# Linear attention with a gated FFN on one core: M3 of two token tiles at the second level, M4's results stored by accumulating DMA

## The chip, the cores and the metric

The kernel runs on one core of a Trainium2 chip. A core has five engines that run their own instruction streams: TensorE (PE, matrix products into PSUM; PEld is its loading of weights), VectorE (DVE), ScalarE (ACT), GpSimd (POOL) and SyncE (SP), which here only issues DMAs. DMAs can be issued by SP, ACT and POOL and run on 16 DMA engines. The metric is the time of one execution on the device in microseconds (us), as the median of the runs shown; a second, profiled execution gives the trace that the readings come from. Times in the trace count from the start of its span.

## The reference

Two blocks are computed from x (2048 tokens of 1024, bfloat16), and one gates the other:

```python
xn = layernorm(x)
q, k, v = split(xn @ wqkv)              # 32 heads of 32
pq, pk  = phi(q), phi(k)                # phi(t) = (t + 1 if t > 0 else exp(t)) + 1e-6
o = (pq @ sum(pk v^T)) / (pq . sum(pk) + 1e-6)
s = o @ wo                              # linear attention
f = (silu(xn @ w_gate) * (xn @ w_up)) @ w_down     # 1024 -> 3584 -> 1024
out = x + s * silu(f)
```

The change concerns the last line and the product with w_down in it.

## The kernel before

The tokens are handled in blocks of 512 (TB), a block in four token tiles of 128 (P). First come the layer norm, the attention and s, which is kept in DRAM as s_dram. Then the FFN runs in two passes of 1024 tokens each (`passes`, the later tokens first). In a pass, gate and up are computed for 14 groups of 256 hidden units (NFG), and then the product with w_down.

All FFN products use the Strassen-Winograd scheme, which replaces the eight block products of a 2x2 by 2x2 block product with seven, M1 to M7, at the price of sums of blocks before and after. For w_down, the rows of a block are 512 tokens, its columns 512 outputs (CW), and the inner dimension is halved by the parity of 128-unit chunks. Tiles 0 to 3 are the first 512 tokens of a pass, tiles 4 to 7 the second; output half 0 is the first 512 columns, half 1 the second. In the last pass, `emit_down_m` (L1459) computes the seven products one after another in the order 1, 2, 6, 7, 5, 4, 3 (M_ORDER). M1, M2, M4 and M7 are done by the same scheme once more, "at the second level" (`l2_M`, L1529): for a pair of token tiles, seven products of seven matmuls with 128 tokens and 256 columns each, in place of 2 x 14 matmuls with 512 columns. Their weight sums were made earlier and lie in DRAM (l2_drams). M6, M5 and M3 are done directly, tile by tile (`prod_t`, L1493: 14 matmuls of 512 columns).

The second level within `l2_M` runs like this, for both tile pairs r = 0, 1: product 1 for both pairs into one half of a PSUM bank; a copy by ACT of each into a second bank (L1538); product 2 onto the first; products 5 and 6; a second copy (L1546); product 7; DVE adds; a `fill()`, which is work of another product for PE; product 4; product 3; DVE adds.

The end of the last pass, which the change rewrites, is:

```python
go(l2_M(4, quads(h, 1, 1), KB, done4, fill3, True))   # fill3: flush(); M3 of tile 0 (out3)
out3(1, 2)                                            # M3 of tile 1, then two stores
ps = banks(2)                                         # two banks for tile 3, preloaded by ACT (L1669)
out3(2, 3)                                            # M3 of tile 2, then three stores
flush()
```

`out3` puts M3 of a tile onto M5 in the same PSUM bank, lets DVE add KA (the running sum of M1, M2, M6 and M7 that output half 1 of tiles 0 to 3 needs), and ACT apply silu. Tile 3 is last and is split into 384 and 128 columns, so that its end is short: there M5 was added to KA early, ACT copies KA into the banks (L1669), and M3 accumulates onto it.

A finished piece of 128 tokens by 512 columns is stored by `fin` (L1219): DVE multiplies silu's result by s (L1223) and adds x (L1224), and SP stores it (L1225). The piece's x and s were loaded into an io tile by `io_load` (L1204; L1214 for x, L1215 for s), which each `fin` calls for a later piece; fq holds the order. Pieces that wait for their `fin` stand in a queue, and `flush(n)` handles n of them.

The order of instructions on PE, DVE, ACT and POOL is the order in which the code emits them; SP's is written by hand in the sections marked so, and otherwise set by the planner. The weights of the seven products are loaded by SP into eight slots (`load_w`, L240; L255 for second-level weights, L262 for M5, M6 and M3), a slot's load being issued when the product that used the slot before has been read. POOL computes the second-level sums of weights and of M1's and M2's left side (L1149, L1180 to L1183) until 673.8 us and is idle after that. DVE makes the left sums of M7 and M4 (`l2_lhs_r`, L1172 to L1175).

Of the kernel before, what the change touches and what calls it, by code (L numbers as in the profile page):

```python
# [21 lines left out]
def kernel(  # L22
# [11 lines left out]
    nc = tc.nc  # L34
# [919 lines left out]
    with ExitStack() as p3:  # L954
# [8 lines left out]
        def k2(shape, dt, name):  # L963
            return kp.tile(shape, dt, name=name, tag="k2")
# [200 lines left out]

        def l2_lhs_r(M, A, r, eng):
            if not isinstance(A, tuple):
                A = (A[:, 0], A[:, 1])
            v = [a.rearrange("p j (r t n) -> p j r t n", r=2, t=2)[:, :, r] for a in A]
            a11, a12, a21, a22 = v[0][:, :, 0], v[1][:, :, 0], v[0][:, :, 1], v[1][:, :, 1]  # L1170
            s1, s2, s3, s4 = [x[:, :, r] for x in l2_bufs(M)]
            eng.tensor_tensor(out=s1, in0=a21, in1=a22, op=ALU.add)  # L1172
            eng.tensor_tensor(out=s2, in0=s1, in1=a11, op=ALU.subtract)
            eng.tensor_tensor(out=s3, in0=a11, in1=a21, op=ALU.subtract)
            eng.tensor_tensor(out=s4, in0=a12, in1=s2, op=ALU.subtract)  # L1175
# [26 lines left out]
        hold = [False]  # L1202

        def io_load(after=None):  # L1204
            if not fq:
                return
            if hold[0] and after is None:
# [6 lines left out]
            gate([nc.sync.dma_start(out=io[:, 0, :], in_=x2[r0:r0 + P, cc * CW:(cc + 1) * CW]),  # L1214
                  nc.sync.dma_start(out=io[:, 1, :], in_=s_dram[r0:r0 + P, cc * CW:(cc + 1) * CW])],  # L1215
                 after, sync=True)
            io_tiles[key] = io

        def fin(p, t, cc, y, eng1, eng2, out_eng, cols=None):  # L1219
            io = io_tiles[(p, t, cc)]  # L1220
            r0 = p * TB2 + t * P
            cs = cols or slice(0, CW)
            eng1.tensor_tensor(out=y[:, cs], in0=y[:, cs], in1=io[:, 1, cs], op=ALU.mult)  # L1223
# [5 lines left out]
        def emit_down(p, h, base, more_S, next_S):  # L1229
# [152 lines left out]
            for hf in range(2):  # L1382
                t0, t1 = 2 * hf, 2 * hf + 1
                for st in range(NS):
                    if st == 4:
                        flush()
                    if hf == 0:
# [71 lines left out]
        def emit_down_m(p, h, base):  # L1459
# [149 lines left out]

            def done2(t, c):  # L1610
                fins.append((t, 0, silu(c, "g11")))
# [36 lines left out]
            tt(KA[-1], M5[-1], KA[-1])  # L1648
            load(5)

            def out3(t, n=0):
                prod_t(3, t, M5[t], False)
                flush(n)
                c = k2([P, CW], FP32, "c12")[:]
                tt(c, M5[t], KA[t])
                fins.append((t, 1, silu(c, "g12")))

            def done4(t, c):
                fins.append((t + TPB, 0, silu(c, "g21")))

            def fill3():
                flush()
                out3(0)
            go(l2_M(4, quads(h, 1, 1), KB, done4, fill3, True))
            hs_ = [slice(0, 3 * CW // 4), slice(3 * CW // 4, CW)]
            out3(1, 2)
# [3 lines left out]
            out3(2, 3)  # L1670
# [194 lines left out]
```

## Time and profile before

| | |
|---|---|
| Median of 3 runs | 751.8 us (751.67 to 751.89) |
| Profiled execution | 751.77 us, span 750.0 us |
| Instructions in the span | 11301 |
| Granted PE clock | 1.000 |
| PE busy from 736.8 to 746.1 us | 9.29 of 9.30 us |
| PE busy from 746.1 us to the end | 0 |
| DMA share, 736.8 to 746.1 us | 0.37 |

The page has the busy time of each engine, the span in 40 slices, the DMA queues, the chain of work that ended last followed back from the last instruction, the costliest groups of instructions, and the DMA issues. A group's row gives the line, the engine, the operation, its output and inputs with shapes, how often, the busy time, the mean of one, and the engine's idle time before it with what ended it. The time line of a stretch gives start and duration, and merges neighbours of the same kind. Matmul ends are modelled: a matmul of 512 columns is shown with 0.379 us, one of 256 with 0.273, while in a row of them the next starts after about 0.216 and 0.109 us.

### The profile page before, as it was taken

The numbers are of one execution on the slowest core, as the hardware profiler recorded it, in microseconds if no ns is written. First come the engines' busy times: TensorE is split into PE (matmuls) and PEld (weight loads), VectorE is DVE, ScalarE is ACT, GpSimd is POOL, SyncE is SP. The second block draws the span as 40 slices with busy tenths as digits, with TensorE's granted clock in tenths as the row PEclk, the third lists the DMA queues.
The fourth block names the chain that finished last, engine by engine and source line by source line (L and its number), as shares of the span: only waits on it lengthen the run. The fifth ranks groups of instructions, "written<-read, shape, count | busy, mean of one in ns | idle before, by whom it ended". The sixth has DMA issues, their size and how long they took to land.

```text
span 750.0 us, 11301 instructions
## 1 busy us (share of the span) xinstructions
PE 743.4 (99%) x3941; PEld 369.6 (49%) x3941; DVE 587.2 (78%) x1068; ACT 384.0 (51%) x553; POOL 398.2 (53%) x492
## 2 busy tenths in 40 slices
PE   8999999999999999999999999999999999999997
PEld 4544544454454444444444444744444444467664
DVE  6687787887697688888889886587877768688856
ACT  5678767889965666666557411232223232332023
POOL 2435799998540255858586027410767575780000
PEclk9999999999999999999999999999999999999999
DMA  9967799869688668787889418898698888679853
GB/s 319 297 148 149 214 331 308 311 141 285 186 212 276 224 228 289 283 317 288 302 281 391 184 55 294 258 375 283 240 307 304 307 295 312 260 229 317 272 186 99
DMA packets 132473, 194.21 MB, mean 259 GB/s; under 512 B 36432, under 2 KB 106192, under 8 KB 122688
## 3 DMA queue, kind: packets, MB, share of 16 engines
q1 hardware_dynamic: 124224, 159.21, 65.9%
q0 software_dynamic: 6752, 31.79, 11.0%
q10 hardware_dynamic: 1440, 2.49, 1.0%
q8 instruction: 31, 0.51, 0.3%
q14 instruction: 26, 0.21, 0.1%
HBM read 122.68 MB, written 63.44 MB: 248 GB/s over the span
## 4 chain that ended last, share of the span: by engine, by line
PE 96%; DVE 3%; ACT 1%; issue 0%; DVEq 0%; ACTq 0%
PE zw L968 26%; PE kv_ps L556 15%; PE xb L968 13%; PE yb L968 6%; PE q_ps L183 6%; PE dzw L1247 6%; PE dm L1526 6%; PE dm L1490 5%; PE s_ps L776 3%; PE fx L818 2%; PE dy L1247 2%; PE dx L1247 2%; PE dm L1247 1%; PE kvz L578 1%; PE nd L745 1%; PE warm_ps L592 1%
## 5 line engine op out<-in xcount | busy, mean ns | idle before, releaser
L968 PEld LDWEIGHTS <-w_sb 128*128 128x128 f16 (+1 forms) x1568 | 152.2, 98 | 182.7
L968 PE MATMUL xb<-xnT,w_sb 128*128 128x512 bf16 x448 | 115.0, 379 | 0.0
L556 PE MATMUL kv_ps<-wkv_sb,xnT 128*128 128x512 bf16 x512 | 113.7, 379 | 0.6 <-DVE xnT L543 0.3
L968 PE MATMUL zw<-xnT,w_sb 128*128 128x512 bf16 x448 | 105.8, 379 | 0.0
L968 PE MATMUL zw<-S,w_sb 128*128 128x512 f16 x448 | 105.8, 379 | 0.0
L323 POOL TENSOR_TENSOR w_sb<-w_sb 128x512 f16<-128x512 bf16 x42 | 50.2, 1195 | 95.7 <-DVE w_sb L311 51.3
L288 ACT ACTIVATE w_sb<-w_sb 128x2048 bf16<-128x2048 bf16 x42 | 79.9, 1902 | 4.7 <-DMA w_sb<-in_B_w_up_dram 4.7
L556 PEld LDWEIGHTS <-xnT 128*128 128x128 bf16 x512 | 48.3, 98 | 56.0 <-ACT xnT L545 0.8
L1149 POOL TENSOR_TENSOR w_sb<-w_sb 128x512 f16<-128x512 f16 (+3 forms) x48 | 51.4, 1093 | 29.0 <-DMA w_sb<-wd 28.0
L1044 ACT ACTIVATE sg<-cg 128x1024 bf16<-128x1024 f32 x28 | 29.6, 1057 | 57.5 <-DVE cg L1037 57.5
L183 PE MATMUL q_ps<-xnT,wq_sb 128*128 128x512 bf16 x256 | 58.4, 379 | 0.0
L968 PE MATMUL yb<-S,w_sb 128*128 128x512 f16 x224 | 57.4, 378 | 0.0
L1037 DVE SCALAR_TENSOR_TENSOR cg<-zw,rc_all,s 128x1024 f32<-128x1024 f32 x28 | 35.9, 1283 | 24.2 <-PE zw L968 12.6
L996 DVE SCALAR_TENSOR_TENSOR s<-yb,rc_all,s 128x512 f32<-128x512 f32 x42 | 31.4, 749 | 29.3 <-ACT s L995 29.3
L324 POOL TENSOR_TENSOR w_sb<-w_sb 128x512 f16<-128x512 bf16 x42 | 50.4, 1201 | 3.3
L1225 POOL DMA_DIRECT2D out_dram<-io x16 | 8.7, 543 | 79.6 <-DVE io L1224 79.4
L326 POOL TENSOR_TENSOR w_sb<-w_sb 128x512 f16<-128x512 bf16 x42 | 50.3, 1197 | 0.0
L325 POOL TENSOR_TENSOR w_sb<-w_sb 128x512 f16<-128x512 bf16 x42 | 50.2, 1196 | 0.0
L995 ACT ACTIVATE s<-xb,rcl 128x512 f32<-128x512 f32 x14 | 9.6, 687 | 65.3 <-PE xb L968 65.3
L995 ACT ACTIVATE s<-xb,rc_all 128x512 f32<-128x512 f32 x42 | 28.3, 674 | 21.9 <-issue 12.9
L311 DVE TENSOR_SCALAR w_sb<-w_sb,cs_all 128x2048 bf16<-128x2048 bf16 x35 | 36.7, 1048 | 2.8
L183 PEld LDWEIGHTS <-wq_sb 128*128 128x128 bf16 x256 | 24.4, 98 | 27.5
(226 smaller groups left out, 1351.4 us busy)
## 6 DMA issues: line engine op xcount, KB each, us to landing
w_sb<-pk_g SPq DMA_DIRECT2D x27, 1024.0 KB, 7.0
pk_g<-w_sb SPq DMA_DIRECT2D x14, 1024.0 KB, 5.4
w_sb<-pk_u SPq DMA_DIRECT2D x14, 1024.0 KB, 8.7
pk_u<-w_sb POOLq DMA_DIRECT2D x13, 1024.0 KB, 5.4
w_sb<-l SPq DMA_DIRECT2D x12, 896.0 KB, 6.6
l<-w_sb POOLq DMA_DIRECT2D x9, 896.0 KB, 7.7
w_sb<-in_B_w_gate_dram SPq DMA_DIRECT2D x14, 512.0 KB, 6.6
w_sb<-in_B_w_down_dram SPq DMA_DIRECT2D x28, 256.0 KB, 4.7
```

What stands on the lines that cost most here:

```text
L183: nc.tensor.matmul(q_ps[:], lhsT=wq_sb[:, dc, g * P:(g + 1) * P], rhs=xn_ap(dc, btok), start=(dc == 0), stop=(dc == DC - 1))
L288: nc.scalar.activation(out=junk, in_=raw_view(key, t), func=ACT.Square, accum_out=asum[:])
L323: nc.gpsimd.tensor_tensor(out=T1, in0=b12, in1=b11, op=ALU.subtract)
L324: nc.gpsimd.tensor_tensor(out=T2, in0=b22, in1=T1, op=ALU.subtract)
L325: nc.gpsimd.tensor_tensor(out=T3, in0=b22, in1=b12, op=ALU.subtract)
L326: nc.gpsimd.tensor_tensor(out=T4, in0=b21, in1=T2, op=ALU.subtract)
L556: mm = nc.tensor.matmul(kv_ps[:], lhsT=xn_ap(dc, tok), rhs=wkv_sb[:, dc, c * CW:(c + 1) * CW], start=(dc == 0), stop=(dc == DC - 1))
L968: mm = nc.tensor.matmul(out, lhsT=lhs(k), rhs=rhs(k), start=(first and k == 0), stop=(k == HK - 1), skip_group_check=True)
L995: nc.scalar.activation(out=s1[:], in_=x_[:], func=ACT.Copy, scale=rc)
L1149: nc.gpsimd.tensor_tensor(out=b(o_), in0=b(a_), in1=b(b_), op=ALU.subtract)
L1247: nc.tensor.matmul(out, lhsT=lhs, rhs=rhs, start=first, stop=lastk, skip_group_check=True)
L1526: nc.tensor.matmul(out, lhsT=lhs, rhs=w[:, j], start=i == 1 and j == 0, stop=j == NQ - 1, skip_group_check=True)
```

## The change

M3 of tiles 0 and 1 is computed at the second level. Its four sums of weights are made by POOL (`t3_sums`, 28 operations of 128x256), out of the slots into which M3's weights were loaded, into the tiles that held S3. Its four left sums are made by DVE (`l3_sums`) into the room of A11. The products go into the banks of M5 of tiles 0 and 1, so M5 of these tiles is now added to KA by DVE beforehand. Products 1, 5, 2 and 6 stand in `fill3`, product 7 after M4, then M3 of tile 2 directly, then products 4 and 3, and tile 3 last as before.

The four pieces of M4 (output half 0 of tiles 4 to 7) are no longer added to x by DVE: x is copied once, DRAM to DRAM, to these rows of out (`acc_base`), and POOL stores each piece with a DMA that accumulates onto out. Their io tiles load s alone.

```diff
--- before.py
+++ after.py
@@ -1163,6 +1163,10 @@
             v = A[:, :, j].rearrange("p k (r t n) -> p k r t n", r=2, t=2)
             return v[:, 0, :, 0], v[:, 1, :, 0], v[:, 0, :, 1], v[:, 1, :, 1]
 
+        def l2_quad4(A):
+            v = [A[:, k].rearrange("p j (r t n) -> p j r t n", r=2, t=2) for k in range(2)]
+            return v[0][:, :, :, 0], v[1][:, :, :, 0], v[0][:, :, :, 1], v[1][:, :, :, 1]
+
         def l2_lhs_r(M, A, r, eng):
             if not isinstance(A, tuple):
                 A = (A[:, 0], A[:, 1])
@@ -1200,6 +1204,11 @@
 
         io_due = deque()
         hold = [False]
+        acc = [(passes[-1], t + TPB, 0) for t in range(TPB)]
+
+        def acc_base():
+            r0 = passes[-1] * TB2 + TB
+            nc.sync.dma_start(out=out2[r0:r0 + TB, 0:CW], in_=x2[r0:r0 + TB, 0:CW])
 
         def io_load(after=None):
             if not fq:
@@ -1211,15 +1220,21 @@
             r0 = p * TB2 + t * P
             pool, tg = (sp, "S%d" % len(fq)) if len(fq) < 3 else (iop, "io")
             io = pool.tile([P, 2, CW], BF16, name="io", tag=tg)
-            gate([nc.sync.dma_start(out=io[:, 0, :], in_=x2[r0:r0 + P, cc * CW:(cc + 1) * CW]),
-                  nc.sync.dma_start(out=io[:, 1, :], in_=s_dram[r0:r0 + P, cc * CW:(cc + 1) * CW])],
-                 after, sync=True)
+            cs = slice(cc * CW, (cc + 1) * CW)
+            loads = [] if key in acc else [nc.sync.dma_start(out=io[:, 0, :], in_=x2[r0:r0 + P, cs])]
+            loads.append(nc.sync.dma_start(out=io[:, 1, :], in_=s_dram[r0:r0 + P, cs]))
+            gate(loads, after, sync=True)
             io_tiles[key] = io
 
         def fin(p, t, cc, y, eng1, eng2, out_eng, cols=None):
             io = io_tiles[(p, t, cc)]
             r0 = p * TB2 + t * P
             cs = cols or slice(0, CW)
+            if (p, t, cc) in acc:
+                eng1.tensor_tensor(out=io[:, 0], in0=y, in1=io[:, 1], op=ALU.mult)
+                nc.gpsimd.dma_start(out=out2[r0:r0 + P, cc * CW:(cc + 1) * CW], in_=io[:, 0], accum_op=ALU.add)
+                io_load()
+                return
             eng1.tensor_tensor(out=y[:, cs], in0=y[:, cs], in1=io[:, 1, cs], op=ALU.mult)
             eng2.tensor_tensor(out=io[:, 0, cs], in0=y[:, cs], in1=io[:, 0, cs], op=ALU.add)
             out_eng.dma_start(out=out2[r0:r0 + P, cc * CW + cs.start:cc * CW + cs.stop], in_=io[:, 0, cs])
@@ -1384,6 +1399,8 @@
                 for st in range(NS):
                     if st == 4:
                         flush()
+                        if hf == 0:
+                            acc_base()
                     if hf == 0:
                         for m in {4: (4,), 8: (5, 6)}.get(st, ()):
                             more_S(m)
@@ -1607,6 +1624,37 @@
                 M5.extend(banks())
                 prod_t(5, 0, M5[0], True)
 
+            T3w = [x[:].rearrange("p j (s n) -> p j s n", s=2) for x in s3_]
+            T3w = dict(zip((5, 6, 7, 4), (T3w[0][:, :, 0], T3w[0][:, :, 1], T3w[1][:, :, 0], T3w[1][:, :, 1])))
+            L3 = A11.bitcast(F16).rearrange("p (j k) (s n) -> p k j s n", k=2, n=P)[:, 0]
+            L3 = dict(zip((5, 6, 7, 3), [L3[:, :, i] for i in range(4)]))
+            Q3 = [v[:, :, 0] for v in l2_quad4(quads(h, 1, 0).bitcast(F16))]
+
+            def w3(j, k, c):
+                return w_of(3, 2 * j + k)[:, c * CH:(c + 1) * CH]
+
+            def t3_sums():
+                for i, k, c, src in ((5, 0, 1, None), (6, 1, 1, 5), (7, 1, 1, None), (4, 1, 0, 6)):
+                    for j in range(NQ):
+                        b_ = w3(j, 0, 0) if i == 5 else w3(j, 0, 1) if i == 7 else T3w[src][:, j]
+                        nc.gpsimd.tensor_tensor(out=T3w[i][:, j], in0=w3(j, k, c), in1=b_, op=ALU.subtract)
+
+            def l3_sums():
+                a11, a12, a21, a22 = Q3
+                tt(L3[5], a21, a22)
+                tt(L3[6], L3[5], a11, ALU.subtract)
+                tt(L3[7], a11, a21, ALU.subtract)
+                tt(L3[3], a12, L3[6], ALU.subtract)
+
+            def l3_p(i):
+                half, y0 = {1: (0, 0), 2: (0, 0), 5: (0, 1), 3: (0, 1), 6: (1, 1), 7: (1, 0), 4: (1, 0)}[i]
+                out = M5[half][:, y0 * CH:(y0 + 1) * CH]
+                for j in range(NQ):
+                    lhs = L3[i] if i in L3 else Q3[{1: 0, 2: 1, 4: 3}[i]]
+                    w = T3w[i][:, j] if i in T3w else w3(j, *{1: (0, 0), 2: (1, 0), 3: (1, 1)}[i])
+                    nc.tensor.matmul(out, lhsT=lhs[:, j], rhs=w, start=i == 1 and j == 0, stop=j == NQ - 1,
+                                     skip_group_check=True)
+
             def done2(t, c):
                 fins.append((t, 0, silu(c, "g11")))
             S3 = tuple(x[:] for x in s3_)
@@ -1645,29 +1693,50 @@
                 fins.append((t + TPB, 1, silu(c, "g22")))
                 if t > 1:
                     flush(1)
-            tt(KA[-1], M5[-1], KA[-1])
             load(5)
-
-            def out3(t, n=0):
-                prod_t(3, t, M5[t], False)
-                flush(n)
-                c = k2([P, CW], FP32, "c12")[:]
-                tt(c, M5[t], KA[t])
-                fins.append((t, 1, silu(c, "g12")))
+            t3_sums()
+            for t in (0, 1, 3):
+                tt(KA[t], M5[t], KA[t])
+            l3_sums()
 
             def done4(t, c):
                 fins.append((t + TPB, 0, silu(c, "g21")))
+            b0, b1 = M5[0:2]
+            lo, hi = slice(0, CH), slice(CH, CW)
 
             def fill3():
                 flush()
-                out3(0)
+                l3_p(1)
+                nc.scalar.copy(out=b1[:, hi], in_=b0[:, lo])
+                l3_p(5)
+                l3_p(2)
+                l3_p(6)
+                nc.scalar.copy(out=b1[:, lo], in_=b1[:, hi])
             go(l2_M(4, quads(h, 1, 1), KB, done4, fill3, True))
             hs_ = [slice(0, 3 * CW // 4), slice(3 * CW // 4, CW)]
-            out3(1, 2)
+            l3_p(7)
+            c1 = k2([P, CW], FP32, "l2c")[:]
+            tt(c1[:, hi], b1[:, lo], KA[1][:, hi])
+            tt(KA[0][:, hi], b1[:, hi], KA[0][:, hi])
+            tt(c1[:, hi], b0[:, hi], c1[:, hi])
+            prod_t(3, 2, M5[2], False)
+            flush(3)
+            c = k2([P, CW], FP32, "c12")[:]
+            tt(c, M5[2], KA[2])
+            g2 = silu(c, "g12")
+            turn[0] += 1
             ps = banks(2)
             for i in range(2):
                 nc.scalar.copy(out=ps[i][:, 0:hs_[i].stop - hs_[i].start], in_=KA[-1][:, hs_[i]])
-            out3(2, 3)
+            l3_p(4)
+            tt(c1[:, lo], b1[:, lo], KA[1][:, lo])
+            g1 = silu(c1, "g12")
+            l3_p(3)
+            flush()
+            c0 = k2([P, CW], FP32, "l2c")[:]
+            tt(c0, b0, KA[0])
+            g0 = silu(c0, "g12")
+            fins.extend([(2, 1, g2), (1, 1, g1), (0, 1, g0)])
             flush()
             t = TPB - 1
             g12 = k2([P, CW], BF16, "g12")[:]
```

## The prediction

> **What bounds the kernel now.** I read the page's busy table first, then the chain of waits over the last 50 us, then the last 35 us engine by engine, because apart from one early copy the change touches only that stretch. The page's first part and the chain, whose columns are start, us, and the work:
>
> ```profile
> PE 743.4 (99%) x3941; PEld 369.6 (49%) x3941; DVE 587.2 (78%) x1068; ACT 384.0 (51%) x553; POOL 398.2 (53%) x492
> ...
> 722.87 0.70 DVE c L1478
> 723.57 0.02 issue
> 723.60 0.72 ACT g L1512
> 724.32 0.28 ACT dm L1538
> 724.60 0.04 issue
> 724.64 6.27 PE dm L1526 x56
> 730.91 3.02 PE dm L1490 x14
> 733.94 3.06 PE dm L1526 x28
> 736.99 8.33 PE dm L1490 x42
> 745.33 0.02 issue
> 745.35 0.59 ACT g L1678
> ```
>
> PE is the path. It leaves it at two places: after 745.33 (silu, multiply, add, store of the last piece: the span ends at 750.0), and once at 722.87, where DVE and then ACT hold PE up. There the copy of M4's first product between two PSUM banks (L1538) stands on ACT behind a silu, that behind a DVE add, and the add waits for the last M5 product. From that product's end (722.85) to PE's next matmul (724.64) are 1.79 us. The chain also gives PE's rates: 14 matmuls of 512 columns take 3.02 us, 28 of 256 take 3.06.
>
> The time line of DVE around 720 and of POOL earlier (start, us of one instruction or group, idle before):
>
> ```profile
> 719.34 0.62 DVE L1175 TENSOR_TENSOR kept<-hT,kept 128x896 f16<-128x896 bf16 x1
> 719.87 0.68 DVE L1478 TENSOR_TENSOR c<-dm,kB 128x512 f32<-128x512 f32 x1
> ...
> 722.87 0.69 DVE L1478 TENSOR_TENSOR c<-dm,kB 128x512 f32<-128x512 f32 x1 [1.53 <-PE dm L1490]
> ```
> ```profile
> 667.41 0.67 POOL L1182 TENSOR_TENSOR w_sb<-hT 128x256 f16<-128x256 bf16 x1
> 668.04 1.44 POOL L1183 TENSOR_TENSOR w_sb<-hT,w_sb 128x256 f16<-128x256 bf16 x1
> 669.45 1.11 POOL L1180 TENSOR_TENSOR kept<-hT 128x256 f16<-128x256 bf16 x1
> ```
> ```profile
> 668.87 4.39 DVE L1478 TENSOR_TENSOR S3h<-hT 128x1024 f16<-128x1024 bf16 x4
> ```
>
> DVE has 1.53 us of slack before the add that holds PE at 722.87, and POOL is idle there. A POOL subtraction of 128x256 takes 0.67 (one per 0.63) alone or beside DVE work that reads PSUM, but 1.1 beside DVE work on two SBUF operands; and those four DVE operations take 1.08 each, where seven of the same size at 681.07, with POOL idle, take 4.29 us, or 0.61 each. So the two engines take turns: 0.61 for DVE, 0.47 for POOL.
>
> **The change part by part.** The sum is made against the profiled execution's 751.77 us (span 750.0, 1.77 around it), 0.03 below the median of 751.8.
>
> *PE work.* M3 of tiles 0 and 1 goes from 28 matmuls of 512 columns (2 x 3.02 = 6.04 us) to 7 x 7 = 49 of 256 (49 / 28 x 3.06 = 5.36). Gain 0.68.
>
> *Wait after M3's product 1.* It goes into one half of bank b0; ACT copies it to b1 (L1710), and the next matmuls, product 5, write b0's other half. In the built order the first load of weights of product 5 waits for ACT: the bank is guarded as a whole. In M4 the same step has two tiles interleaved, so that a second product covers the copy; here there is one tile pair, and nothing. Price: the last matmul of 256 columns lasts 0.27 at a pitch of 0.11, so 0.16 drains; 0.02 to ACT; 0.36 copy (L1546's mean); 0.04 back: 0.58. Bounds 0.28 (PE's idle at 724.36, with cover) and 0.7; I take 0.58, which is built of this very step. The second copy (L1714) has 3.06 us of M4's products after it and costs nothing.
>
> *Wait before the last tile.* The copies of KA into the last tile's two banks (L1730, before L1669) used to stand on ACT at 741.70, ahead of need at 742.87. They now stand behind the silu of tile 2, which waits for the DVE add on tile 2's product, the same three steps as at 722.87. There PE was back 1.79 after the product ended; here the copy is of 384 columns (L1669: 0.47, not 0.36), so 1.90. PE has products 4 and 3 of M3 to do meanwhile: 14 x 0.109 = 1.53, less 0.16 of drain, 1.37. PE stands for 0.53. Bounds 0.1 (a copy that started at once) and 0.9; I take 0.53. Product 4 and product 3 wait for POOL and DVE work that is long done.
>
> *POOL's 28 subtractions (L1640).* Their data land when M3's slots do: the eight loads of L262 are issued from 712.27 to 717.1 and take 4.5 to 5.2 us, so slab 0 is there at about 717.25 and one more every 0.7 us to 721.6. The first seven sums thus fall on DVE's second set of M4's sums (L1172 to L1175, 717.61 to 719.95) and on the two operations of a final store. Taking turns at 0.47 per POOL operation, I step through it: the four sums end at 721.4 instead of 719.9, the store's two operations at 723.3, and the add that had 1.53 us of slack starts at 723.33 instead of 722.87. Silu, copy and PE behind it move as far: 0.46. Bounds 0 (one collision hidden) and 1.1. Going on like this, the sums for products 5, 6, 7 and 4 are complete at 724.0, 730.3, 735.9 and 740.5; PE, on the times of this sum, wants the last of each at 733.2, 734.7, 738.5 and 742.4. POOL is covered by 1.9 us at its tightest, a mean of 0.83 us against 0.90 allowed.
>
> The Trainium skill, "SBUF — State Buffer", section "Who interferes with whom", says that a DVE instruction with two SBUF inputs contends with a GpSimd one that reads SBUF, and that the loser blocks for the whole instruction. The trace agrees on which instructions collide, but its pair takes 1.08, less than the 0.61 + 0.63 of whole blocking; what the sum would be by the rule's letter stands as a rival below.
>
> *DVE's additions.* Two more adds onto KA (0.60 pitch) and four sums of 128x896 (0.54, 1.0 beside POOL) stand in DVE's idle 5.3 us before 730.26; they end at 730.7 and delay M4's adds by half a microsecond, which PE reads only at 734. M4's results lose one of two DVE operations each. In the end three stores instead of two stand between the last-but-one product and the last: 0.60 + 3 x 0.87 = 3.2 us from 0.35 before PE starts the last tile, so done 2.9 after that start (742.87 in the trace), while ACT's silu of the first piece ends 3.1 after it (745.93). Cost 0, with 0.2 to spare.
>
> *DMAs.* SP loses four loads of x and four stores in the tail; nothing waited there for SP. POOL issues four accumulating stores: three behind its last sum at 741, one at about 744, while the last SP store lands near 748.7 + 0.9. Nothing on POOL stands behind them. No row shows an accumulating transfer; POOL's plain stores of the same 128 KB land 2.0 to 6.4 us after issue (median 3.4), and one more read of 128 KB takes 2.6 in this stretch (the loads of x), so 746 to 753; I take 750, at the edge, and count 0. The Trainium skill, "DMA: Bandwidth & Descriptors", section "Rules for kernel authors", says that an accumulate reads its destination and writes it later, which is that added read; no run here shows it yet.
>
> *The copy of x to out.* It is written in the first pass, but the built order has it on SP right after the loads of wq, so at 23 us. 512 KB at the 349 GB/s of that stretch are 1.5 us, or 3.0 if reading and writing share it:
>
> ```profile
> 28.00:30.50 2.50, 2.50 (x19) 1.37 (x18) 2.37 (x5) 2.50 (x6) 2.09 (x6) 1.00 1.10 349
> ...
> 31.50:33.50 2.00, 2.00 (x17) 1.15 (x16) 1.97 (x5) 1.91 (x4) 1.39 (x7) 1.00 0.05 15
> ```
>
> The last two columns are the DMA engines' share and GB/s: full until 30.5, empty from 31.5 to 33.5. The transpose behind it (L530) is issued at 32.39, when DVE is ready, and lands about 3.3 later; PE reads that tile at 38.5 (eight matmuls, 1.73 us, before the next group of L578 at 40.29). 2.8 us of slack against at most 1.5 of delay: cost 0.
>
> *Sum:* -0.68 + 0.58 + 0.53 + 0.46 = +0.89. 751.77 + 0.89 = 752.7, or 0.12% more. From no change, a measurement of this kernel can tell about 0.2%, or 1.5 us: 750.3 to 753.3.
>
> **The rivals.**
>
> *The gain stays.* The copy's wait is shorter than its parts, and the order on ACT does no harm: 751.77 - 0.68 = 751.1. For it: only that such handoffs sometimes overlap. Against it: the built order has both waits. A gain above 1.5 us has no source, since all of M3's saving is 0.68.
>
> *DVE held off for all of each POOL operation*, 0.63 instead of 0.47: the same stepping has the add before M4 start at 724.16 instead of 723.33, 0.83 more, and POOL's last sum end at 743.4, about when PE then wants it: 753.5. For it, the 1.44 us of one POOL row; against it, the 1.08 of the pairs. It is what the Trainium skill's section named above would give.
>
> *POOL late for product 4* (the case on the slower side): if DVE keeps POOL at the 1.07 of the collision rows throughout, 28 take 30.0 us, to 747.2, and PE, which wants the last at 742.4, stands for 4.8: 757.5. It decides from a mean of 0.90 us on. Against it: DVE's work on two SBUF operands fills only 9 of these 24 us (eight sums of 0.54, eight store operations of 0.42, four results of 0.35).
>
> *The accumulating store ends the kernel.* The last, issued at 744, decides if it takes over 5.6 us to land; at 9.0 (6.4 + 2.6) the end moves by 3.4: 756. Against it: plain stores land in 1.8 in this stretch, where DMA is at a third.
>
> **How the numbers follow.** Forecast 0.47 (its own range 752.0 to 753.3), gain stays 0.08, whole blocking 0.18, POOL late 0.11, late store 0.12, something else 0.04. Slower by over 0.2%: 0.18 + 0.11 + 0.12, 0.01 of the forecast's upper edge and half of the rest, 0.44. Faster: 0.02 of the kept gain, should more come with it, and 0.01 of the rest, 0.03. Within: what is left, 0.53. The range from 751.2 to 755.5 takes in the forecast, most of the kept gain, the blocking and the milder half of the late cases.
>
> **What would show it.** PE idle 0.6 after the first seven matmuls of L1655, released by ACT L1710; idle 0.5 before the 384-column matmuls, released by L1730; the DVE add before M4 at about 723.3, and PE's wait there 0.7 instead of 0.28; L1640's POOL rows at 0.83 on average and done by 741. The prediction is wrong if a matmul of L1655 waits for POOL, if SP's last wait is for POOL's queue, or if PE idles near 38.

## The result and the profile after

The changed kernel takes 753.14 us (median of 9 runs, 752.97 to 755.61) where the kernel before takes 751.62 (9 runs, 751.34 to 751.89): a ratio of 1.0025, with an interval of 1.0015 to 1.0036. It is slower by 1.5 us. The forecast was 752.7 us, and the range of 751.2 to 755.5 holds the time; but the likeliest case, less than 0.2% from no change, is just missed by the median, and the interval reaches into it.

The profiled execution takes 753.14 us with a span of 751.1, so 2.04 lie around the span; before, it was 751.77, 750.0 and 1.77. First the page's busy times, the trace's waits of PE over the last 50 us, and the time line of PE around each of them (start, us, and in brackets the idle time before with what ended it):

```profile
PE 743.0 (99%) x3962; PEld 371.4 (49%) x3962; DVE 595.6 (79%) x1073; ACT 384.9 (51%) x555; POOL 424.4 (57%) x524
```
```profile
PE dm L1543 <- ACT dm L1555: 0.8, 1, 0.8
PE dm L1655 <- DVE kB L1495: 0.5, 1, 0.5
PE dm L1507 <- ACT dm L1730: 0.4, 1, 0.4
```
```profile
722.73 1.69 PE L1543 MATMUL dm<-w_sb,hT 128*128 128x256 f16 x14
725.23 1.03 PE L1543 MATMUL dm<-w_sb,hT 128*128 128x256 f16 x8 [0.81 <-ACT dm L1555]
...
731.34 0.93 PE L1655 MATMUL dm<-w_sb,hT 128*128 128x256 bf16 x7
732.81 0.93 PE L1655 MATMUL dm<-S3h,hT 128*128 128x256 f16 x7 [0.54 <-DVE kB L1495]
733.57 0.93 PE L1655 MATMUL dm<-w_sb,hT 128*128 128x256 bf16 x7
...
742.71 0.93 PE L1655 MATMUL dm<-w_sb,hT 128*128 128x256 bf16 x7
744.08 2.71 PE L1507 MATMUL dm<-w_sb,hT 128*128 128x384 bf16 x19 [0.45 <-ACT dm L1730]
```

In the kernel before, PE had one wait here, of 0.28 us:

```profile
724.64 1.69 PE L1526 MATMUL dm<-w_sb,hT 128*128 128x256 f16 x14 [0.28 <-ACT dm L1538]
```

Now there are three, and they are the three of the forecast: before M4, after M3's product 1, and before the last tile. The rows give their price from start to start. Seven matmuls of 256 columns that follow each other take 0.76 (732.81 to 733.57). Product 5 starts 1.47 after product 1, so 0.71 are lost; the last tile starts 1.37 after product 3, so 0.61; and M4's fourteen matmuls take 2.50 to the next start instead of 1.97 (722.67 to 724.64), so 0.53. That is 1.85; M3 itself saves 0.69, as two later runs show; PE is 0.06 late already at 722.7. So the last tile should start 1.22 later, and the trace has it at 744.08 instead of 742.87.

The chain of waits (start, us) returns to PE through the same add, silu and copy as before, 0.6 later, and leaves it once more ahead of the last tile. (Before, the chain left PE only at 722.85, when the add's product was done; now it leaves PE at 713.08 and runs along DVE's queue from there. Between the two pieces shown it also names DVE additions for the wait after product 1, which the part on the prediction takes up.)

```profile
723.48 0.69 DVE c L1495
...
724.19 0.72 ACT g L1529
724.91 0.28 ACT dm L1555
...
725.23 6.27 PE dm L1543 x56
...
742.14 0.70 DVE c L1495
...
742.93 0.45 ACT g L1529
...
743.56 0.48 ACT dm L1730
...
744.08 2.45 PE dm L1507 x14
```

Both pieces have one form: a copy that PE needs stands on ACT behind a silu, and the silu waits for a DVE add that PE does not need. (L1529 is the silu, L1555 and L1730 are the copies.) The time line of DVE and of POOL in the stretch where the first add is delayed:

```profile
718.31 0.98 DVE L1177 TENSOR_TENSOR kept<-kept,hT 128x896 f16<-128x896 f16 x1
719.21 1.08 DVE L1178 TENSOR_TENSOR kept<-hT 128x896 f16<-128x896 bf16 x1
720.22 1.08 DVE L1179 TENSOR_TENSOR kept<-hT,kept 128x896 f16<-128x896 bf16 x1
...
723.48 0.68 DVE L1495 TENSOR_TENSOR c<-dm,kB 128x512 f32<-128x512 f32 x1
```
```profile
717.87 6.22 POOL L1640 TENSOR_TENSOR S3h<-w_sb 128x256 f16<-128x256 bf16 x7 [44.03 <-DVE c L1495]
...
735.14 4.80 POOL L1640 TENSOR_TENSOR S3h<-w_sb,S3h 128x256 f16<-128x256 bf16 x7
740.93 2.74 POOL L1235 DMA_DIRECT2D out_dram<-io  x3 [0.98 <-DVE io L1234]
743.96 0.87 POOL L1235 DMA_DIRECT2D out_dram<-io  x1 [0.29 <-DVE io L1234]
```

DVE's sums take 0.98 to 1.08 us beside POOL's, and the add starts straight behind DVE's queue at 723.48, with no idle time before it, where it had 1.53 us.

### The profile page after: what moved, and what is told of

Same layout as the page of the kernel before. It is cut to its first block, busy times and chain, and to the rows that moved or that the text cites. A ratio compares the mean times of both kernels' runs of the same rounds, so it can differ in the third digit from the quotient of the medians.

```text
span 751.1 us, 11394 instructions
## 1 busy us (share of the span) xinstructions
PE 743.0 (99%) x3962; PEld 371.4 (49%) x3962; DVE 595.6 (79%) x1073; ACT 384.9 (51%) x555; POOL 424.4 (57%) x524
## 4 chain that ended last, share of the span: by engine, by line
PE 95%; DVE 3%; ACT 1%; issue 0%; DVEq 0%; ACTq 0%
PE zw L968 26%; PE kv_ps L556 15%; PE xb L968 13%; PE yb L968 6%; PE q_ps L183 6%; PE dzw L1262 6%; PE dm L1543 5%; PE fx L818 3%; PE dm L1507 3%; PE s_ps L776 3%; PE dy L1262 2%; PE dx L1262 2%; PE dm L1262 1%; PE kvz L578 1%; PE nd L745 1%; PE warm_ps L592 1%
```

## The experiments

Theory: the three waits of PE make the loss inside the span, each by its own mechanism (DVE and POOL taking turns; a bank guarded as a whole; the order on ACT). Rivals: the accumulating stores or the copy of x make it; DVE's work in the last 20 us does; or something around the span. Times are medians of 5 to 11 runs, each compared with the kernel before on the same chip. The same few tenths of a microsecond separate many of these runs, so the waits in the traces carry more than the medians do.

**Without POOL's sums.**

```diff
-            t3_sums()
```

> The changed kernel without GpSimd's 28 weight sums: M3 of tiles 0 and 1 multiplies by what the slots hold (this part of the result is left out), all else stays. Theory (POOL and DVE take turns, and that delays the add before M4): the DVE work of L1176 to L1179 takes 0.62 us again where it took 0.98 to 1.08, the add that started at 723.48 starts at about 722.9, PE's wait before M4 falls from 0.81 us to about 0.28, and the other two waits of PE (0.45 to 0.5 each) stay: the span falls by 0.5 to 0.6, from 751.1 to about 750.55, and the time from 753.14 to about 752.6. Rival 1 (the add is late for another reason, a load or the order on DVE): it still starts at 723.4 or later, time 753.1. Rival 2, on the time around the span, which went from 1.77 to 2.04 us: if POOL working until 740 makes it, it falls back to about 1.8 as well and the time is 752.35; if the accumulating stores make it, it stays at 2.0.

752.22 us, ratio 1.0008 (0.9999 to 1.0017). DVE's time line and PE's waits:

```profile
717.97 0.62 DVE L1177 TENSOR_TENSOR kept<-kept,hT 128x896 f16<-128x896 f16 x1
...
722.58 0.69 DVE L1495 TENSOR_TENSOR c<-dm,kB 128x512 f32<-128x512 f32 x1 [1.52 <-PE dm L1507]
```
```profile
PE dm L1655 <- ACT dm L1709: 0.4, 1, 0.4
PE dm L1507 <- ACT dm L1729: 0.4, 1, 0.4
PE dm L1543 <- ACT dm L1555: 0.3, 1, 0.3
```

DVE's operations are back at 0.62, the add has its 1.52 us of slack again, and the wait before M4 is the one of the kernel before. So the sums make what that wait has grown by, and rival 1 is out. More was gained than forecast (1.0 instead of 0.5 to 0.8): the time around the span is 1.79, as before the change, and the wait after product 1 is 0.1 shorter, which the part on the prediction takes up.

**Sums of 16 columns instead of 256.**

```diff
-                        nc.gpsimd.tensor_tensor(out=T3w[i][:, j], in0=w3(j, k, c), in1=b_, op=ALU.subtract)
+                        nc.gpsimd.tensor_tensor(out=T3w[i][:, j, 0:16], in0=w3(j, k, c)[:, 0:16], in1=b_[:, 0:16],
+                                                op=ALU.subtract)
```

> The changed kernel with GpSimd's 28 sums kept as instructions, with the same waits and in the same order, but each over 16 columns instead of 256 (240 of every 256 columns of the summed weights are left out, so the result of tiles 0 and 1 is too). Two questions. The wait before M4: if the time for which POOL shares the SBUF port with DVE makes it, the DVE operations of L1177 to L1179 are back at 0.62 us, the wait at 0.28 and the span at 750.4 as without the sums; if each collision costs a fixed amount, they stay near 1.0. The time around the span, 2.0 us with both sums and accumulating stores and 1.74 to 1.8 without either: if the mere number of POOL instructions (524) or their waits make it, it stays at 2.0 and the time is 752.4; if it is POOL's work until 740, it falls to 1.8 and the time is 752.2.

752.51 us, ratio 1.0010 (1.0001 to 1.0020). The DVE operations of L1177 to L1179 take 0.62 to 0.63, and the wait before M4 is 0.3: DVE loses by how long POOL's operations last, not by a price for each meeting. Around the span it stays at 2.01, although POOL has no sum left after 725.5. So it is not the length of the sums, nor that they run until 740, that costs this time.

**M4's results stored as before.**

```diff
-        acc = [(passes[-1], t + TPB, 0) for t in range(TPB)]
+        acc = []
...
-                        if hf == 0:
-                            acc_base()
```

> The changed kernel with M4's results stored as before the change: x is loaded, DVE multiplies and adds, plain stores; no copy of x to the output and no accumulating store. M3's second level and the 28 sums stay. Theory (the three waits of PE make all of the loss inside the span): PE's waits stay at 0.81, 0.5 and 0.45, the span at 751.1 within 0.2. DVE has four more additions of about 0.42, which delay the add before M4 at most a little, since those stores lie behind it. Around the span: if the accumulating transfers make the 2.04 us instead of 1.77, it goes back to about 1.8 and the time is 752.9; if GpSimd's late work makes it, it stays and the time is 753.1. Rival (the copy of x and the accumulating stores cost the time, in the first pass or in the tail): the span falls to 750.2 and the time to 752.0 or less.

753.34 us, ratio 1.0022 (1.0013 to 1.0030), a span of 751.4, and 1.74 around it.

```profile
PE dm L1505 <- ACT dm L1728: 0.9, 1, 0.9
PE dm L1541 <- ACT dm L1553: 0.8, 1, 0.8
PE dm L1653 <- DVE kB L1493: 0.5, 1, 0.5
```

The copy of x and the accumulating stores do not make the loss: without them all three waits are there, and the one before the last tile is longer. There the add on tile 2's product stands behind three stores of two DVE operations each, and starts at 742.34, without idle time before it. So inside the span the accumulating stores save something (0.3 us in the profiled executions, 0.5 by the medians of the spans), and around it they cost 0.26 (2.00 against 1.74 on average).

**Only the accumulating stores, with M3 as before.**

```diff
+            tt(KA[-1], M5[-1], KA[-1])
             load(5)
-            t3_sums()
-            for t in (0, 1, 3):
-                tt(KA[t], M5[t], KA[t])
-            l3_sums()
...
+            def out3(t, n=0):
+                prod_t(3, t, M5[t], False)
...
-                l3_p(1)
...
+                out3(0)
```

> The kernel before, with M3 as it was (three 512-column products, no weight sums), but M4's results stored by accumulating DMA onto the early copy of x. Theory: the copy of x at 23 us and the accumulating stores cost nothing inside the span, and the 0.22 us that the changed kernel spends more around its span needs both the sums and the accumulating stores (without the sums it was 1.78, without the accumulating stores 1.77, with both 2.0): the span is that of before within 0.2 (749.8 to 750.2), the time within 0.2 of before, at about 751.7. Rival: the copy of x delays the first pass, or the accumulating transfers cost in the tail: 752.0 or more. Second rival: two DVE operations less per result let the tail end earlier: 751.4.

751.61 us, ratio 0.9998 (0.9989 to 1.0007), with PE's only wait again 0.28 and 1.80 around the span. By themselves the stores and the copy cost nothing and bring nothing. The longer time around the span is seen only where the 28 sums and the four accumulating stores come together (1.97 to 2.01 on average in eight kernels, the changed one among them; 1.74 to 1.81 in the six with neither or with one of them). These kernels also differ in how many instructions POOL has, 524 in the eight and 492 to 520 in the six, and no run separates the number from the kind.

**A cover for the copy after product 1.**

```diff
                 nc.scalar.copy(out=b1[:, hi], in_=b0[:, lo])
+                for k in range(NWA):
+                    mm(3, 2, k, M5[2], False)
                 l3_p(5)
...
-            prod_t(3, 2, M5[2], False)
+            for k in range(NWA, NFG):
+                mm(3, 2, k, M5[2], False)
```

> The changed kernel with seven of the fourteen 512-column matmuls of M3's tile 2 put right behind M3's product 1; the other seven stay where they were. Theory (PE waits for the ACT copy L1710, since bank b0 is guarded as a whole): the seven matmuls last 1.5 us and the copy with its handoffs 0.6, so the wait of 0.5 us (0.70 start to start) in the middle of L1655 goes; the tile's result comes at the same time as before, since its last seven matmuls stay, but PE's other work between it and the last tile is the same 1.5 us, so the wait before the last tile stays at about 0.45. Span from 751.1 to about 750.45, time from 753.14 to about 752.45. Rival (the page names the DVE add kB that ended at 732.81, not the copy, as what PE waited for): the wait stays behind the seven matmuls or comes back before product 5 only if that add is later than 733.5; if DVE were the cause, product 5 would follow 1.5 later and the wait would be gone too, but the DVE add would then be seen to end after the copy and just before PE resumes, and PE would have stood at product 5 in either order with a later add. If PE loses as much elsewhere, 753.1.

752.86 us, ratio 1.0015 (1.0006 to 1.0024). PE's time line:

```profile
731.17 0.93 PE L1655 MATMUL dm<-w_sb,hT 128*128 128x256 bf16 x7
731.93 1.67 PE L1507 MATMUL dm<-w_sb,hT 128*128 128x512 bf16 x7
733.45 0.93 PE L1655 MATMUL dm<-S3h,hT 128*128 128x256 f16 x7
...
743.77 3.05 PE L1507 MATMUL dm<-w_sb,hT 128*128 128x384 bf16 x25 [1.00 <-ACT dm L1733]
```

The wait after product 1 is gone, as the theory has it. But the wait before the last tile grew from 0.45 to 1.00, which I had not expected; the time was to be 752.45. Tile 2's product is now ready sooner than DVE: its add starts at 741.84 directly behind six additions and three accumulating stores' multiplications, with no idle time, where in the changed kernel DVE had waited 0.86 for the product. The copies of KA stand behind that add's silu.

**The copies of KA ahead of tile 2's product.**

```diff
+            turn[0] += 1
+            ps = banks(2)
+            for i in range(2):
+                nc.scalar.copy(out=ps[i][:, 0:hs_[i].stop - hs_[i].start], in_=KA[-1][:, hs_[i]])
             prod_t(3, 2, M5[2], False)
...
-            turn[0] += 1
-            ps = banks(2)
-            for i in range(2):
-                nc.scalar.copy(out=ps[i][:, 0:hs_[i].stop - hs_[i].start], in_=KA[-1][:, hs_[i]])
```

> The changed kernel with the two ACT copies of KA into the last tile's banks issued ahead of M3's tile 2, so that on ACT they stand in front of that tile's silu and no longer behind it. Theory: the copies end well before PE needs them, the wait of 0.45 us (0.61 start to start) ahead of the 384-column matmuls goes, and the other two waits of PE stay; span from 751.1 to about 750.5, time from 753.14 to about 752.55. Rival (the banks are freed late, by the DVE add that read them last, so that the copies have to wait there and hold up the silu behind them): the wait stays at 0.4 or more and the end may slip, 753.1 to 753.6. A second rival: DVE's tail (0.42 us of idle before the first operation of the last piece came from ACT) ends later than PE's gain lets it, so that only 0.2 to 0.4 of the 0.6 reaches the end: 752.8.

752.61 us, ratio 1.0011 (1.0002 to 1.0019). PE goes from product 3 to the last tile without a wait (its row at 743.13 follows product 3's 742.36 by 0.77); the other two waits are as they were. This is the gain that was expected, 0.6. From 742.56 on, though, DVE has no idle time to the end, and its last piece waits for DVE, no longer for ACT.

**Two of DVE's stores moved out of the crowded stretch.**

```diff
-                if t > 1:
-                    flush(1)
             load(5)
```

> The changed kernel without the two stores that DVE makes between the results of the second tiles of M5 (the pieces are stored later, when DVE is idle). GpSimd's sums stay and still collide with the second set of M4's sums. Theory (turns of POOL and DVE use up 1.5 us of DVE's slack and then 0.5 to 0.6 more, and any 1.1 us of DVE work that is taken out of the stretch gives it back): two operations of 0.85 to 0.92 beside POOL go, so the add before M4 starts when its product is there, 0.6 earlier than in the changed kernel; PE's wait there falls from 0.81 to 0.28; span 750.5, time about 752.5, unless PE then waits at the last tile for a DVE that has the moved stores to do, which would take back up to 0.4 (752.9). Rival (the add is held by the sums themselves, by a whole operation each, not by the queue of work): the add stays at least 0.3 late and the wait at 0.6 or more, 753.

754.03 us, ratio 1.0034 (1.0022 to 1.0047): slower than the change itself. PE's waits, and the DVE rows that carry it:

```profile
PE dm L1507 <- ACT dm L1728: 1.7, 1, 1.7
PE dm L1655 <- POOL S3h L1640: 0.5, 1, 0.5
PE dm L1543 <- ACT dm L1555: 0.3, 1, 0.3
```
```profile
723.21 0.69 DVE L1495 TENSOR_TENSOR c<-dm,kB 128x512 f32<-128x512 f32 x1 [1.02 <-PE dm L1507]
...
737.31 0.88 DVE L1238 TENSOR_TENSOR g<-g,io 128x512 bf16<-128x512 bf16 x1
738.23 0.77 DVE L1239 TENSOR_TENSOR io<-g,io 128x512 bf16<-128x512 bf16 x1
738.93 1.94 DVE L1495 TENSOR_TENSOR l2c<-dm,kB 128x256 f32<-128x256 f32 x4
```

The theory holds where it was meant: the add has slack again, and the wait before M4 is 0.28. (In the second line of waits POOL is named, but its sums for product 5 were done at 724.0; the copy after product 1 is what ended last there.) But the stores, now four in a row where the changed kernel has two, run from 732.59 to 739.0, beside POOL's later sums, at 0.76 to 0.89 an operation, and M4's and M3's additions queue behind them. Besides, an io tile is freed later, so a load of s lands only at 742.19. Moving DVE work off one path put it on the next: "when DVE is idle", as I had written, is little after 731 (0.99, 0.86 and 0.42 us in the changed kernel), and none of it lies where the stores went.

**All three, with and without accumulating stores.** The three edits above together:

```diff
-                if t > 1:
-                    flush(1)
...
                 nc.scalar.copy(out=b1[:, hi], in_=b0[:, lo])
+                for k in range(NWA):
+                    mm(3, 2, k, M5[2], False)
...
+            ps = banks(2)
+            for i in range(2):
+                nc.scalar.copy(out=ps[i][:, 0:hs_[i].stop - hs_[i].start], in_=KA[-1][:, hs_[i]])
-            prod_t(3, 2, M5[2], False)
+            for k in range(NWA, NFG):
+                mm(3, 2, k, M5[2], False)
```

> All three repairs in the changed kernel: tile 2's first seven matmuls behind product 1, the copies of KA ahead of its last seven, and the two stores of M5's stretch later. Theory: the three waits of PE go (0.6 + 0.7 + 0.6 start to start), leaving M3's gain of 0.68: span 751.1 - 1.8 = 749.3, and with the 2.0 around it 751.3, against 751.7 before, ratio 0.9995. Putting tile 2 behind product 1 alone gave only 0.36, since the wait before the last tile grew from 0.45 to 1.0: that tile's add was queued behind DVE's other adds and stores; here the copies no longer depend on it, so the full 0.7 should come. Rival (DVE's work in the last 20 us has become the bound, so that each wait that is taken from PE comes back as a later end of DVE): the span stays at 750.0 or more and the time at 752.0 or more, with PE's waits gone but DVE without idle time from 735 on.

and the same with `acc = []` and without `acc_base()`:

> The same three repairs, and M4's results stored as before, without accumulating stores and without the copy of x. Theory: as with the accumulating stores inside the span, if DVE has room for its four more additions of 0.42, and 0.22 less around it: 749.3 + 1.77 = 751.1, ratio 0.999. Rival (DVE is the bound of the last 20 us: without the accumulating stores alone the wait before the last tile rose from 0.45 to 0.9 us): the four additions make the end 0.4 to 1.7 later, 751.5 to 752.8, and the accumulating stores are what pays for the second level there.

With the accumulating stores: 753.42 us, ratio 1.0022 (1.0013 to 1.0031). Without: 754.56, ratio 1.0040 (1.0027 to 1.0053). Both went the rival's way, and the second beyond the 752.8 at which the rival ended. PE's waits after product 1 and before the last tile are gone, but a new one of 0.61 stands before product 4, for a DVE add onto KA, and the span stays at 751.0 and 752.8. From 738 on the time line has DVE idle only once in each, for 0.40 and 0.54 us, and its four more additions (1.7 us) make the span 1.4 longer by the medians of the two: DVE is now the bound.

**The silu behind the copies.** PE never needed the late add or its silu, only the copies behind them on ACT. One line moves:

```diff
-                fins.append((t + TPB, 1, silu(c, "g22")))
+                if t < TPB - 1:
+                    fins.append((t + TPB, 1, silu(c, "g22")))
...
-            go(l2_M(4, quads(h, 1, 1), KB, done4, fill3, True))
+            m4_ = l2_M(4, quads(h, 1, 1), KB, done4, fill3, True)
+            next(m4_)
+            fins.append((2 * TPB - 1, 1, silu(c, "g22")))
+            go(m4_)
```

> The changed kernel with one line moved: the silu of M5's last tile is issued on ACT after M4's first two bank copies instead of ahead of them; DVE's late add and its queue stay as they are. Theory: PE never needed that add or that silu, only the copy of M4's product 1 that stood behind them on ACT, so PE's wait before M4 goes from 0.81 us to 0.28 or nothing although the DVE add is still at about 723.3 to 723.5: span 751.1 - 0.7 = 750.4, time from 753.14 to about 752.4. Rival (DVE's total work in the last 30 us bounds the end, as the run with three repairs suggests, where waits that were taken from PE came back): DVE's additions of M4 keep their place at 731.1, so up to 0.5 of the gain comes back as a wait for DVE or ACT before the last tile (0.45 grows to about 0.9), time 752.9.

752.33 us, ratio 1.0003 (0.9994 to 1.0012), span 750.4. DVE's add is as late as ever (723.66, in an execution that is 0.2 later at that point), but PE runs through:

```profile
722.90 3.22 PE L1543 MATMUL dm<-w_sb,hT 128*128 128x256 f16 x28
```

So before M4 DVE's lateness costs PE time only through ACT's order, and the fix of one line gets back what POOL's sums took there.

**All three waits away, no store moved; and the one line alone in the kernel before.** The repaired change has the moved silu, the cover and the early copies of KA; in the kernel before, only the silu moves (the first of these edits):

```diff
+            next(m4_)
+            fins.append((2 * TPB - 1, 1, silu(c, "g22")))
...
                 nc.scalar.copy(out=b1[:, hi], in_=b0[:, lo])
+                for k in range(NWA):
+                    mm(3, 2, k, M5[2], False)
...
+            ps = banks(2)
+            for i in range(2):
+                nc.scalar.copy(out=ps[i][:, 0:hs_[i].stop - hs_[i].start], in_=KA[-1][:, hs_[i]])
-            prod_t(3, 2, M5[2], False)
+            for k in range(NWA, NFG):
+                mm(3, 2, k, M5[2], False)
```

> The changed kernel with all three waits of PE taken away without moving any of DVE's stores: the silu of M5's last tile behind M4's first copies, tile 2's first seven matmuls behind M3's product 1, the copies of KA ahead of its last seven. Theory: 0.8 + 0.7 + 0.6 = 2.1 us of PE's path go, span 749.0 and, with 2.0 around it, time 751.1, ratio 0.999. DVE had 1.85 us of idle time between 730.7 and the end of its work with the early copies (0.99 and 0.86), so 0.3 may be lost to it: 751.4. Rival (DVE is the bound): no more comes than with the early copies alone, 752.6, with DVE without idle time from 731 on and PE's waits gone or turned into waits for DVE.

> The kernel before with the same one line moved: the silu of M5's last tile behind M4's first two bank copies. Theory: PE's only wait there, 0.28 us, goes, and nothing else stands in the way: span 749.7, time 0.3 less than before, at about 751.4. Rival (PE still waits for a copy, since the copy takes 0.36 and tile 1's product covers it only in part): 0 to 0.1 less, 751.65. It says whether a repaired version of the change beats a kernel before that has had the same line moved.

The repaired change takes 751.90 us, ratio 0.9999 (0.9990 to 1.0008); the kernel before with the moved line 751.42, ratio 0.9996 (0.9986 to 1.0005). The first was to be 751.1 to 751.4 and missed that, the second came as expected. Neither can be told from the kernel before, and the repaired change is not faster than the kernel before with the same line moved: by the medians it is 0.5 us slower, 0.3 in the span and 0.2 around it, which the intervals do not separate. In both PE has no wait left in the last 50 us, so M3's own gain can be read from the last rows of PE and DVE, of the repaired change first:

```profile
742.00 3.22 PE L1507 MATMUL dm<-w_sb,hT 128*128 128x384 bf16 x28
...
746.40 0.23 DVE L1239 TENSOR_TENSOR io<-g,io 128x128 bf16<-128x128 bf16 x1
```
```profile
736.46 9.26 PE L1490 MATMUL dm<-w_sb,hT 128*128 128x512 bf16 x56
...
746.52 0.23 DVE L1224 TENSOR_TENSOR io<-g,io 128x128 bf16<-128x128 bf16 x1
```

PE ends at 745.22 instead of 745.72, in an execution whose M4 starts 0.19 later (722.93 against 722.74): 0.69 saved, the 0.68 of the forecast. At DVE's last operation 0.12 of the 0.50 is left (it ends at 746.63 against 746.75, with no more than 0.58 us of idle time from 731 on), and the span is longer, 749.9 against 749.6. The traces put this last part down to the DMA engines. The answers on DMA over 744 to 748 us, of the repaired change and of the unaltered kernel before:

```profile
q0 software_dynamic: 408, 0.37, 69.5%
q1 hardware_dynamic: 627, 0.50, 37.9%
...
out_dram<-io POOLq DMA_DIRECT2D x1, 128.0 KB, 4.7
...
out_dram<-io SPq DMA_DIRECT2D x1, 32.0 KB, 2.0
```
```profile
q1 hardware_dynamic: 584, 0.50, 38.3%
...
out_dram<-io SPq DMA_DIRECT2D x1, 32.0 KB, 1.5
```

The columns of a queue are packets, MB and share of 16 engines; of an issue, its size and the us to landing. The accumulating queue (q0) has packets until 747, and the engines' share is 0.97 to 1.14 in each microsecond from 743 to 747, where it is 0.38 to 0.47 in the kernel before. The plain stores of SP lie among these packets, and the last one, with which the kernel ends, lands after 2.0 instead of 1.5 (1.5 in the kernel before with the moved line as well). That is read from traces: no run has the repaired change with its stores in place and without accumulating.

## Why the prediction was right or wrong

- *PE work, -0.68*: right, measured -0.69.
- *Wait after product 1, 0.58*: the mechanism was right (the cover takes it away), the size was 0.71. The drain (0.16) and the copy (0.36) were as counted, the step to ACT was 0.04 instead of 0.02. The way back was counted as 0.04, as at M4, and was 0.14. In the changed kernel's trace a semaphore instruction of 0.05 us of its own stands in PE's queue there, and with the sums of 16 columns too (idle 0.54 in both). In the kernel without the sums it is not there, and the idle time is 0.45. That it is there because product 5 must also wait for POOL is likely, not shown. The page's name for this wait, a DVE add, is a coincidence of ends: in the two runs with altered sums the same wait is put down to ACT's copy.
- *Wait before the last tile, 0.53*: right, measured 0.61; the three steps took 1.97 instead of 1.90. The early copies take it away.
- *POOL's sums, 0.46*: right, measured 0.53. The add started at 723.48 (forecast 723.33). The sums averaged 0.79 us (forecast 0.83) and were done at 739.94 (forecast 740.5); PE stood still for none of them.
- *DVE's additions, 0*: right for the change, where DVE's last piece had 0.42 of idle time before it. But "0.2 to spare" was the warning that I did not follow up: with PE's waits repaired, DVE was the next bound, and 0.38 of the 0.69 us that M3 saves on PE got no further than DVE.
- *DMAs, 0, and the copy of x, 0*: right inside the span; PE has no wait from 15 to 60 us. The accumulating stores were issued at 740.93 and 743.96 (forecast 741 and 744) and landed in about 3.7 us, where I took 6.
- *What lies around the span* was carried over at 1.77 and was 2.04. This is the step that failed: about 0.25 of the 0.5 us by which the forecast was too low, and without it the change would have stayed within 0.2%. (The other half is the sizes of the three waits, too small by 0.13, 0.08 and 0.07.) In the runs it comes only with the 28 sums and the accumulating stores together, and the sums' length does not matter (16 columns do it too). Whether it is the two kinds together or the 524 POOL instructions that they add up to, no run tells, nor why: nothing of that time is in the trace.

*The rivals.* That the gain stays: no, all the waits came. Whole blocking, as the Trainium skill has it ("SBUF — State Buffer", "SBUF: two separate sides"): the instructions that it names did collide, but a DVE operation of 0.62 took 1.08 at most, not 0.61 + 0.63, so turns are the better reading. The time alone would not tell: 753.14 is nearer to this rival's 753.5 than to 752.7. The rows do: the add started at 723.48 and not at 724.16, and POOL's sums ended at 739.94 and not at 743.4. POOL late: no wait for it. The accumulating store ends the kernel: not in the change, where the accumulating queue has drained by 747 and the last plain store, of 32 KB, lands after 1.6; in the repaired version, by its trace, it delayed the stores that do.

## What to carry to other kernels

When an engine's queue mixes work that the bound engine needs with work that it does not, the second kind passes every delay on to the first: look for the copy behind the silu before looking for a faster add, since moving one line gave what moving DVE's stores could not. A saving on the bound engine is worth only the slack of the next engine in that stretch; here, of 0.69 us on PE, 0.31 came through at DVE's last operation, and the stores behind it shared the DMA engines with slower ones. And of a change of a tenth of a per cent, also the time around the span has to be read, run by run.

## What the hardware showed unexpectedly

- Packets of an accumulating store last almost three times as long on record as plain ones. Between 744 and 746 us the changed kernel's accumulating queue and the kernel before's plain stores move the same bytes:

```profile
q0 software_dynamic: 287, 0.26, 116.9%
```
```profile
q1 hardware_dynamic: 274, 0.26, 39.0%
```

  1.169 x 16 x 2 us / 287 = 130 ns a packet, against 0.390 x 16 x 2 / 274 = 46 ns. A share above 100% means that the recorded packets overlap, so 130 ns is what one lasts and not what it costs: 287 packets in 16 x 2 us leave at most 111 ns for each. The Trainium skill ("DMA: Bandwidth & Descriptors", "Rules for kernel authors") says that an accumulate reads its destination and writes it later; the longer packets fit that, though the trace does not show what an engine does within one.
- POOL is busy for 0.87 us with issuing one accumulating store of 128 KB and for 2.74 with three, and they land 3.2 to 4.3 us after issue, where SP's plain ones of that size take 1.7 or 1.8 in the kernel before.
- Where product 5 has POOL's sums as an input, a semaphore instruction of 0.05 us of its own stands in PE's queue, and the matmul follows ACT's copy 0.14 us after its end; without the sums it is 0.05.
- The time around the span went from 1.80 to 2.0 us by 28 small GpSimd operations together with four accumulating stores, and by neither alone; the cause is open.
